# Attention scores on two halves of the matrix engine's rows, a third score buffer, and expert tiles planned around the transposes

## The chip, the cores and the metric

One core of a Trainium2 chip runs the whole kernel. The metric is the device time of one execution, in microseconds. The engines are PE (matrix multiplication; weights are loaded by PEld beside it), DVE (vector), ACT (activation functions), POOL and SP; the last two, with ACT, also issue DMAs. Matmuls write to PSUM, which has eight banks of 512 fp32 columns.

## The reference

An attention layer whose queries are pooled in pairs, followed by a layer of experts in which each row belongs to one expert, named by `domain_id`.

```python
q_pool = q.reshape(B, H, S // 2, 2, D).mean(axis=3)
scores = scale * np.matmul(q_pool, k.transpose(0, 1, 3, 2))
scores = scores - np.max(scores, axis=-1, keepdims=True)
attn = np.exp(scores)
attn = attn / (np.sum(attn, axis=-1, keepdims=True) + 1e-09)
x = np.matmul(attn, v)            # then (B, H, S/2, D) -> (B*S/2, H*D)
...
h = np.maximum(x[mask] @ w1[e], 0.0)   # for each expert e
out[mask] = h @ w2[e]
```

B = H = 8, S = 1152 keys and 576 pooled queries, D = 64; 4608 rows of 512, 8 experts with an inner width of 1024.

## The kernel before

**Attention.** Two heads make a pair; there are 32 pairs (`NPAIR`), four to a batch. The scores are computed transposed, keys on partitions, so that their exponentials are at once the stationary operand of the product with v. The 9 x 576 columns of a pair are cut into 12 steps (`SPP`) of 432 columns for both heads. `score(t)` writes a step into one of two PSUM buffers `s` (each two banks, one per head): for each head a matmul over all 128 rows, where the keys of both heads lie on the partitions (`kq`) and the queries (`qz[p % 2][r]`) are zero in the other head's 64 rows. `expo(t)` lets ACT take the exponential of both heads' 432 columns, without a maximum (reference: the rows' maximum is subtracted). `av(p, c)` multiplies one block of 128 keys with v for both heads, ten matmuls of 65 columns, the last of which holds the sum; both heads accumulate in one tile `acc` of two banks. `evac(p)` divides by the sum on DVE. `turn_k` and `turn_q` transpose k and q of the next pair on PE into the bank `tp`, from where DVE copies them.

**Experts.** When the first batches are done, their rows go to HBM (`put_x`), are gathered by expert (`get_x`, an indirect DMA on POOL, 128 rows a tile), turned and multiplied. An expert has five tiles (`NTC`, 640 slots), eight experts 40 tiles. Some tiles are computed during attention, in pieces of four matmuls of 128 columns (`up`) or one of 512 (`down`), with the bank `m`; their rows are turned by a transposing DMA (`flip_x`). The others run after it, in the tail, in `runs` of one to five tiles: `stage1` (w1 and ReLU, 32 matmuls for each stretch of columns) and `stage2` (w2, eight matmuls of 512 columns a tile), then a scatter by POOL. Runs under five tiles take their rows by `flip_x`, runs of five by `turn_tile` on PE.

**What sets the order.** The order is written out by a planner while the program is built: a loop over steps t, which issues scores, exponential, the value products that are due (`AVS`), transposes at steps 3 and 7 of a pair, and then as many expert pieces as fit: each kind of work is charged a number of nanoseconds (`C_S` 370 for a step's scores, `C_AV` 315 for ten value matmuls, `C_TK` 460, `C_TQ` 420, 216 for a piece), a step has `STEP` 769, and a piece is issued while the overrun stays under `LAG`. Each engine runs its instructions in that order. Weights of five experts (`HELD`) are loaded during attention on POOL's queue at the steps `WANT`, those of the last three in the tail. q comes by SP's queue, k and v by POOL's.

## Time and profile before

| | |
|---|---|
| median of three runs | 451.21 us (450.73 to 452.18) |
| span of the profiled execution | 456.6 us |
| attention, first to last exponential | 8.69 to 317.93 us |
| tail, from the first steady expert matmul to PE's last | 319.60 to 449.70 us |
| PE, ACT busy | 433.2, 345.8 us |
| DVE, POOL busy | 221.5, 163.3 us |
| tiles of 40 computed during attention | 6 |

The trace is one execution under the profiler. Its span, from the first to the last instruction, is the own time that it shows; it is 1.2% above the median of the runs without profiler. A row of a timeline gives the start, the time to the end of the last instruction, engine, line, operation, output and inputs and the count; in brackets the idle time before it and what ended it. PE's matmuls overlap: a row's time is longer than the distance between starts.

### The profile page before, as it was taken

The numbers are of one execution on the slowest core, as the hardware profiler recorded it, in microseconds if no ns is written. First come the engines' busy times: TensorE is split into PE (matmuls) and PEld (weight loads), VectorE is DVE, ScalarE is ACT, GpSimd is POOL, SyncE is SP. The second block draws the span as 40 slices with busy tenths as digits, with TensorE's granted clock in tenths as the row PEclk, the third lists the DMA queues.
The fourth block names the chain that finished last, engine by engine and source line by source line (L and its number), as shares of the span: only waits on it lengthen the run. The fifth ranks groups of instructions, "written<-read, shape, count | busy, mean of one in ns | idle before, by whom it ended". The sixth has DMA issues, their size and how long they took to land.

```text
span 456.6 us, 13089 instructions
## 1 busy us (share of the span) xinstructions
PE 433.2 (95%) x5568; PEld 307.1 (67%) x5568; DVE 221.5 (49%) x558; ACT 345.8 (76%) x457; POOL 163.3 (36%) x275
## 2 busy tenths in 40 slices
PE   7999999999999999999999999998979998999993
PEld 4777777777877877777777777776534545555551
DVE  4588778786554644544644554542222222333230
ACT  5999999999999999999999999998212222333221
POOL 5311241212610322644431441300646855732413
PEclk9999999999999999999999999999999999999998
DMA  8995699998999987999987799800564899941203
GB/s 204 243 249 90 109 254 228 186 243 174 184 235 234 211 147 163 231 230 235 199 170 145 158 226 210 189 13 24 140 148 134 174 244 178 236 165 71 93 8 112
DMA packets 62854, 78.61 MB, mean 172 GB/s; under 512 B 19695, under 2 KB 48880, under 8 KB 62786
## 3 DMA queue, kind: packets, MB, share of 16 engines
q0 software_dynamic: 35200, 50.31, 57.7%
q1 hardware_dynamic: 27314, 27.25, 24.6%
q8 instruction: 45, 0.74, 0.7%
q14 instruction: 23, 0.19, 0.1%
q10 hardware_dynamic: 272, 0.13, 0.1%
HBM read 95.46 MB, written 15.21 MB: 242 GB/s over the span
## 4 chain that ended last, share of the span: by engine, by line
ACT 46%; PE 31%; issue 10%; DMA 6%; POOL 4%; DVE 1%; POOLq 1%; another core or an unknown queue 1%
ACT e L599 46%; PE s L587 11%; DMA w2h<-in_moe_w_dram 6%; PE acc L610 6%; PE hp L986 5%; PE op L1019 4%; POOL out_dram L504 3%; PE acc L160 1%; PE m L768 1%; PE m L781 1%; PE tp L550 1%; PE tp L564 0%; DVE hT L993 0%; POOLq L1046 0%
## 5 line engine op out<-in xcount | busy, mean ns | idle before, releaser
L599 ACT ACTIVATE e<-s 128x864 f16<-128x864 f32 x384 | 305.9, 893 | 3.8 <-PE s L587 2.7
L587 PE MATMUL s<-qz,kq 128*128 128x432 f16 (+2 forms) x1152 | 203.1, 284 | 6.3 <-ACT e L599 4.4
L610 PEld LDWEIGHTS <-e 128*128 128x128 f16 x2880 | 120.5, 97 | 25.6 <-DVE xb L624 8.9
L610 PE MATMUL acc<-v,e 128*128 128x65 f16 x2880 | 134.3, 193 | 0.3 <-ACT e L599 0.3
L587 PEld LDWEIGHTS <-kq 128*128 128x128 f16 x1152 | 97.5, 97 | 33.0 <-issue 12.1
L504 POOL DMA_INDIRECT out_dram<-osb,gid x40 | 40.8, 1019 | 84.9 <-DVE osb L787 41.5
L111 POOL DMA_DIRECT2D vs<-in_v_dram x32 | 23.8, 743 | 114.0 <-DVE v L529 66.7
L1019 PE MATMUL op<-w2h,hT 128*128 128x512 f16 x272 | 62.1, 379 | 1.8 <-DVE hT L993 1.8
L648 POOL DMA_INDIRECT xs<-x_tok,grow x40 | 40.9, 1022 | 63.7 <-DVE xs L91 42.2
L986 PE MATMUL hp<-xt,w1h 128*128 128x384 f16 (+3 forms) x384 | 56.5, 304 | 5.6 <-issue 3.1
L986 PEld LDWEIGHTS <-w1h 128*128 128x128 f16 x416 | 36.7, 98 | 31.6 <-issue 6.0
L993 DVE TENSOR_SCALAR hT<-hp 128x384 f16<-128x384 f32 (+2 forms) x40 | 24.4, 611 | 60.1 <-PE hp L986 39.4
L571 DVE COPY qz<-tp 64x576 f16<-64x576 f16 x62 | 28.2, 456 | 51.3 <-PE tp L564 47.2
L1025 ACT COPY osb<-op 128x512 f32<-128x512 f32 x21 | 12.3, 586 | 53.1 <-PE op L1019 44.5
L991 ACT ACTIVATE hT<-hp 128x384 f16<-128x384 f32 (+2 forms) x40 | 21.2, 534 | 40.3 <-PE hp L986 35.5
L1019 PEld LDWEIGHTS <-hT 128*128 128x128 f16 x272 | 25.9, 98 | 30.6 <-DVE hT L993 2.8
L623 DVE RECIPROCAL rr<-acc 128x10 f32<-128x10 f32 x32 | 7.1, 221 | 50.6 <-PE acc L610 47.7
L520 DVE TENSOR_TENSOR qp<-q 96x768 f16<-96x768 f32 x31 | 29.3, 946 | 1.0 <-DMA q<-in_q_dram 0.9
L624 DVE TENSOR_TENSOR xb<-acc,rr 128x640 f16<-128x640 f32 x32 | 26.4, 824 | 1.1
L120 POOL DMA_DIRECT2D k<-in_k_dram x31 | 23.1, 744 | 7.0 <-DVE q L91 4.3
L1027 DVE COPY osb<-op 128x512 f32<-128x512 f32 x13 | 9.0, 692 | 32.3 <-PE op L1019 29.4
L554 DVE COPY kq<-tp 128x1024 f16<-128x1024 f16 x31 | 21.2, 683 | 3.5 <-PE tp L550 3.5
(129 smaller groups left out, 292.4 us busy)
## 6 DMA issues: line engine op xcount, KB each, us to landing
q<-in_q_dram SPq DMA_DIRECT2D x31, 576.0 KB
vs<-in_v_dram POOLq DMA_DIRECT2D x32, 288.0 KB
k<-in_k_dram POOLq DMA_DIRECT2D x31, 288.0 KB
w1h<-in_moe_w_dram POOLq DMA_DIRECT2D x16, 512.0 KB
w2h<-in_moe_w_dram POOLq DMA_DIRECT2D x16, 512.0 KB
x_tok<-xb SPq DMA_DIRECT2D x23, 96.0 KB
x_tok<-xb SPq DMA_DIRECT2D x22, 64.0 KB
x_tok<-xb SPq DMA_DIRECT2D x23, 32.0 KB
```

Source lines behind the costliest of these rows:

```text
L111: nc.gpsimd.dma_start(vs[:, :, :, :], v[b, h : h + 2].rearrange("h (p c) d -> p h c d", p=P))
L504: ins = nc.gpsimd.indirect_dma_start(out=dst[:, :], out_offset=bass.IndirectOffsetOnAxis(ap=ap, axis=0), in_=src, in_offset=None, **kw,)
L520: nc.vector.tensor_tensor(out=qp[:, :, :, :].rearrange("p j h d -> p h j d"), in0=q2[:, :, :, 0:D], in1=q2[:, :, :, D : 2 * D], op=ALU.add,)
L571: nc.vector.tensor_copy(qz[p % 2][r][lo : lo + 64, :], mt[lo : lo + 64, P : P + Sp])
L587: nc.tensor.matmul(s[:, r, o : o + n], lhsT=kq[p][:, c * P : (c + 1) * P], rhs=qz[p % 2][r][:, q0 : q0 + n], start=True, stop=True,)
L599: nc.scalar.activation(e_[:, :, o : o + W], st.pop(t)[:, :, 0:W], AF.Exp, bias=0.0, scale=0.0625)
L610: nc.tensor.matmul(acc[p][:, h, i * (D + 1) : (i + 1) * (D + 1)], lhsT=e_[:, h, o + QO[i] : o + QO[i] + P], rhs=v16[p % NV][:, c, h, 0 : D ...
L624: nc.vector.tensor_tensor(out=xb[b][:, :, 2 * hp * D : 2 * (hp + 1) * D].rearrange("p i (h d) -> p h i d", h=2), in0=a[:, :, :, 0:D], in1= ...
L648: nc.gpsimd.indirect_dma_start(out=dst, out_offset=None, in_=x_dram[0 : 1 + nb * Sp, :], in_offset=bass.IndirectOffsetOnAxis(ap=ap, axis=0),)
L986: nc.tensor.matmul(hp_[:, lo : lo + n], lhsT=w1h[:, cc, f * P : (f + 1) * P], rhs=xt[:, cc, lo : lo + n], start=cc == 0, stop=cc == ND - 1,)
L993: nc.vector.tensor_scalar(out=hT[:, f, 0:m], in0=hp_[:, 0:m], scalar1=0.0, scalar2=None, op0=ALU.max)
L1019: nc.tensor.matmul(op_[:, :], lhsT=hT[:, f, i * P : (i + 1) * P], rhs=w2h[:, f, :], start=f == 0, stop=f == NF - 1,)
```

## The change

**Scores.** `score` now issues, for each stretch of columns, one matmul on partitions 0 to 63 and one on 64 to 127 (`HALF`): each head uses its own 64 rows of the array, and the queries `qz[p % 2]` of both heads lie in one tile without zeros. Each head's result goes to its own bank. There are three `s` buffers (six banks); `acc` is one bank, used by the first head's nine blocks and then by the second's (`av(p, h, c, pool)`, `evac(p, h)`), and one bank `px` serves everything else.

**Transposes.** `turn` replaces `turn_k` and `turn_q`: 30 transposes of 64 rows, into an `s` buffer in its turn, and three DVE copies.

**Order.** Two items (two steps, or a step and a transposition) are issued as a window at the first one's step, followed by value products in groups of 15 and expert pieces. The charges are new (`C_S` 183, `C_AV` 147 for five, `C_T` 440, `C_P` 217, and `C_MODE` 190 for a window), with exceptions for the windows around the transposes (`SPAN`).

**Experts.** Five experts (`FILL`) instead of three have tiles filled in; rows are turned on PE in attention (`turn_x`) and in the tail. Six experts' weights are held, the sixth in space that q's load buffers leave (`wlast`); the last two are loaded two pieces a run. q of the pairs from the fifth on is loaded by POOL's queue, one pair earlier.

**Checks.** The reciprocals of all sums are kept; `check_sums` counts on the chip those out of a range, and if any is, a general path (`again`) recomputes all with the rows' maxima. It lies behind a branch at the program's end, where there was one for experts with over 640 rows.

```diff
-    NFX = 14
+    NFX = 10
...
-    ering = att.enter_context(tc.tile_pool(name="ering", bufs=3))
+    ering = att.enter_context(tc.tile_pool(name="ering", bufs=4))
...
-    spsum = att.enter_context(tc.tile_pool(name="spsum", bufs=2, space=bass.MemoryType.PSUM))
+    spsum = att.enter_context(tc.tile_pool(name="spsum", bufs=3, space=bass.MemoryType.PSUM))
     apsum = att.enter_context(tc.tile_pool(name="apsum", bufs=1, space=bass.MemoryType.PSUM))
-    tpsum = att.enter_context(tc.tile_pool(name="tpsum", bufs=1, space=bass.MemoryType.PSUM))
-    mpsum = att.enter_context(tc.tile_pool(name="mpsum", bufs=1, space=bass.MemoryType.PSUM))
+    xps = att.enter_context(tc.tile_pool(name="xps", bufs=1, space=bass.MemoryType.PSUM))
...
-            nc.sync.dma_start(
+            (nc.sync if p < 4 else nc.gpsimd).dma_start(
...
+    def turn(p):
+        kp, qp = kpt[p], qpt[p]
+        new_kq(p)
+        mt = spsum.tile([P, 2, 512], FP32, name="s")[:, :, :].bitcast(F16)
+        for c in range(NC + NJ):
+            src = kp[:, c, :, :] if c < NC else qp[:, c - NC, :, :]
+            for r, (lo, hi) in enumerate(HALF):
+                nc.tensor.transpose(
+                    mt[:, r, c * 64 : c * 64 + 64],
+                    in_=src[lo:hi, :, :].rearrange("p h d -> p (h d)"),
+                    identity=ident16[lo:hi, lo:hi],
+                )
...
-            for r in range(2):
+            for r, (lo, hi) in enumerate(HALF):
                 nc.tensor.matmul(
-                    s[:, r, o : o + n], lhsT=kq[p][:, c * P : (c + 1) * P],
-                    rhs=qz[p % 2][r][:, q0 : q0 + n], start=True, stop=True,
+                    s[:, r, o : o + n], lhsT=kq[p][lo:hi, c * P : (c + 1) * P],
+                    rhs=qz[p % 2][lo:hi, q0 : q0 + n], start=True, stop=True,
                 )
...
+    WSTEP = [[20 + 44 * e + 11 * j for j in range(4)] for e in range(4)]
+    WSTEP.append([236 + 13 * j for j in range(4)])
+    WSTEP.append([(NPAIR - 3) * SPP + 10 + 3 * j for j in range(4)])
...
+    AVS = [
+        {at: [(g // 3, c, ACC) for c in range(3 * (g % 3), 3 * (g % 3) + 3)] for g, at in enumerate(ats)}
+        for ats in ((9, 11, 13, 15, 17, 19), (9, 11, 13, 15, 16, 19))
+    ]
+    AVS_END = {
+        8: [(0, c, ACC) for c in range(4)],
+        10: [(0, c, ACC) for c in range(4, 6)],
+        12: [(0, c, ACC) for c in range(6, NC)],
+        13: [(1, c, ACC) for c in range(NC)],
+    }
+    STEP, C_MODE, C_S, C_T, C_AV, C_X, C_P, LAG = 771, 190, 183, 440, 147, 220, 217, 250
+    SPAN = ({2: 1270, 4: 1700, 5: 880}, {3: 1200, 5: 1500, 6: 1150})
+    FILL, HELD = 5, len(WSTEP)
...
+        def able(self, t):
+            b = self.blocks[0] if self.blocks else None
+            return b and (b[3] or b[4].get("t", NST) < t < NST - 14 and t >= WSTEP[b[4]["xs"][0]][3] + 14)
...
-    for e, i in [(e, i) for i in range(NA) for e in range(HELD - 2)]:
+    early = [(0, 0), (1, 0), (2, 0), (3, 0), (0, 1), (1, 1), (2, 1), (3, 1), (4, 0), (4, 1)]
+    for e, i in early + [(e, 2) for e in range(FILL)]:
         add_tile(e, i)
...
+        if s_ == (10 if p == 0 else 7 if p == 1 else 4) and p + 1 < NPAIR:
+            items.append(-(p + 1))
+    windows = {}
+    for i in range(0, len(items), 2):
+        w = items[i : i + 2]
+        windows[w[0] if w[0] >= 0 else w[1]] = w
...
+        for it in windows.get(t, ()):
+            if it < 0:
+                turn(-it)
+                work_ns += C_T
+            else:
+                score(it)
+                expo(it)
+                work_ns += C_S
+                span += STEP
+        if span:
+            work_ns += C_MODE
+            span = SPAN[p % 2].get(s_, span) if p > 1 else span
...
+            room = (180 if p > 1 and s_ in SPAN[p % 2] else LAG) + span - debt - work_ns
...
-                if j1 - j0 < NTC:
-                    flip_x(dst, en, j)
-                else:
-                    btw.append(lambda dst=dst, j=j: turn_tile(dst, xs[en, j], j))
+                btw.append(lambda dst=dst, en=en, j=j: turn_tile(dst, xs[en, j], j))
...
+        h = stage1(wts[e][0], xt[k_], n * P, {**at, 2: part, 7: part})
...
+        if k_ == 3:
+            check_sums()
+        if i1 == NTC and e in (0, 3) and rest:
```

PE, in the middle of attention (pair 17 and about). Before, one expert matmul (`m<-w2h`), then a step's scores and the first transpose:

```order
L610 LDWEIGHTS e
L610 MATMUL acc<-v_1_104,e 128x65
L781 LDWEIGHTS h_4043
L781 MATMUL m<-w2h,h_4043 128x512
L587 LDWEIGHTS kq
L587 MATMUL s<-qz_0_99,kq 128x432
L587 LDWEIGHTS kq
L587 MATMUL s<-qz_1_100,kq 128x432
L550 LDWEIGHTS kp
L550 MATMUL tp<-ident_106,kp 128x128
```

After, at a like place, a window of two steps (the last of one pair, the first of the next), with the buffers' numbers kept:

```order
L814 LDWEIGHTS h0_4866
L814 MATMUL px_5108<-w2h_1377,h0_4866 128x512
L594 LDWEIGHTS kq_4723
L594 MATMUL s_5118<-qz_0_96,kq_4723 128x432
L594 LDWEIGHTS kq_4723
L594 MATMUL s_5118<-qz_0_96,kq_4723 128x432
L594 LDWEIGHTS kq_4975
L594 MATMUL s_5122<-qz_1_97,kq_4975 128x432
L594 LDWEIGHTS kq_4975
L594 MATMUL s_5122<-qz_1_97,kq_4975 128x432
L615 LDWEIGHTS e_4973
L615 MATMUL acc_5092<-v16_0_100,e_4973 128x65
```

Two steps' scores stand together, both halves of a step read the same q tile, and value products and expert matmuls lie between windows.

DVE, at the transposes of a pair. Before, the evacuation of both heads (`rr`, `xb`), then the copies of k (`kq`) and of the zero-padded q (`qz`):

```order
L623 RECIPROCAL rr<-acc 128x10
L624 TENSOR_TENSOR xb<-acc,rr 128x2x5x64
L91 MEMSET xs 1x1
L554 COPY kq<-tp 128x1024
L571 COPY qz_0_101<-tp 64x576
L571 COPY qz_1_102<-tp 64x576
L572 COPY kq<-tp 128x128
```

After, for one head (its sums' reciprocals are kept in `cum`), then the copies from a score buffer:

```order
L628 RECIPROCAL cum<-acc 128x5
L630 TENSOR_TENSOR xb<-acc,cum 128x5x64
L570 COPY kq<-s 128x2x9x64
L575 COPY qz_97<-s 128x6x64
L575 COPY qz_97<-s 128x6x32
```

The evacuation is half as wide and comes twice a pair, and the three copies free a score buffer.

ACT, from the last exponential into the tail; `hT<-hp` is ReLU, its columns the run's rows, `osb<-op` a finished tile, `xt<-hp` turned rows. Before:

```order
L599 ACTIVATE e<-s 128x2x432 x384
L991 ACTIVATE hT<-hp 128x384 x4
L1025 COPY osb_7117<-op 128x512
L1025 COPY osb_7147<-op 128x512
L991 ACTIVATE hT<-hp 128x384 x4
```

After:

```order
L606 ACTIVATE e<-s 128x2x432 x384
L1048 ACTIVATE hT<-hp 128x384 x4
L1082 COPY osb_8037<-op 128x512
L1082 COPY osb_8067<-op 128x512
L1048 ACTIVATE hT<-hp 128x128 x4
L1082 COPY osb_8150<-op 128x512
L1048 ACTIVATE hT<-hp 128x128 x4
L1067 COPY xt<-hp 128x4x128
L1082 COPY osb_8239<-op 128x512
L1048 ACTIVATE hT<-hp 128x256 x4
```

Before, five runs of three tiles, two of two and three of five follow; after, one of three, two of one, six of two and two of five.

## Rows read from the trace of the kernel before

**Rows 1.** The page's first line.

```profile
span 456.6 us, 13089 instructions
```

**Rows 2.** Three windows: stretch, length, busy time (count) by engine, clock, DMA.

```profile
19.08:113.37 94.29, 92.14 (x1458) 71.97 (x1455) 73.82 (x224) 94.29 (x121) 21.53 (x32) 1.00 0.98 195
113.37:317.90 204.53, 201.68 (x3203) 158.07 (x3199) 100.84 (x218) 201.91 (x253) 66.47 (x101) 1.00 0.90 179
319.60:449.70 130.10, 122.45 (x744) 65.98 (x744) 36.51 (x80) 35.59 (x67) 65.60 (x118) 1.00 0.63 146
```

**Rows 3.** Timeline: start, time, engine, line, operation; POOL and ACT at a stall.

```profile
289.09 1.02 POOL L648 DMA_INDIRECT xs<-x_tok,grow  x1 [0.27 <-issue]
...
290.56 1.67 ACT L599 ACTIVATE e<-s 128x864 f16<-128x864 f32 x2 [0.66 <-PE s L587]
```

**Rows 4.** Groups by shape, 100 to 200 us: count, busy us, mean ns, idle before.

```profile
L587 PE MATMUL s<-qz,kq 128*128 128x432 f16 x126 | 33.1, 344 | 0.8 <-ACT e L599 0.4
```

**Rows 5.** Timeline of PE around 153 us.

```profile
152.30 0.47 PE L610 MATMUL acc<-v,e 128*128 128x65 f16 x10
...
152.61 0.38 PE L768 MATMUL m<-xt,w1h 128*128 128x128 f16 x4
...
152.83 0.53 PE L587 MATMUL s<-qz,kq 128*128 128x288 f16 x4
...
153.50 0.53 PE L587 MATMUL s<-qz,kq 128*128 128x432 f16 x2
...
153.87 0.61 PE L550 MATMUL tp<-ident,kp 128*128 128x128 f16 x8
...
154.34 0.53 PE L587 MATMUL s<-qz,kq 128*128 128x432 f16 x2
```

**Rows 6.** Timeline of PE in the tail, one row for each width.

```profile
343.25 5.36 PE L986 MATMUL hp<-xt,w1h 128*128 128x384 f16 x32
...
376.55 1.69 PE L986 MATMUL hp<-xt,w1h 128*128 128x256 f16 x14
...
403.89 0.39 PE L1004 MATMUL hp<-ident,xs 128*128 128x128 f16 x4
...
440.78 8.80 PE L1019 MATMUL op<-w2h,hT 128*128 128x512 f16 x40
```

**Rows 7.** Groups by shape, 318 to 457 us: the closing matmuls.

```profile
L1019 PE MATMUL op<-w2h,hT 128*128 128x512 f16 x272 | 62.1, 379 | 1.8 <-DVE hT L993 1.8
```

**Rows 8.** Timeline of PE in the tail's second run.

```profile
333.90 0.81 PE L986 MATMUL hp<-xt,w1h 128*128 128x384 f16 x4 [1.78 <-issue]
335.29 0.81 PE L986 MATMUL hp<-xt,w1h 128*128 128x384 f16 x4 [0.58 <-issue]
336.77 1.46 PE L986 MATMUL hp<-xt,w1h 128*128 128x384 f16 x8 [0.68 <-DVE xs L91]
```

**Rows 9.** Timeline at the end of attention.

```profile
316.25 1.68 ACT L599 ACTIVATE e<-s 128x864 f16<-128x864 f32 x2
...
317.99 0.45 PE L610 MATMUL acc<-v,e 128*128 128x65 f16 x9 [0.34 <-ACT e L599]
...
318.27 0.81 PE L986 MATMUL hp<-xf,w1h 128*128 128x384 f16 x4
...
318.73 0.82 DVE L624 TENSOR_TENSOR xb<-acc,rr 128x640 f16<-128x640 f32 x1
...
319.61 0.66 PE L986 MATMUL hp<-xf,w1h 128*128 128x384 f16 x3 [0.52 <-DVE xb L624]
```

**Rows 10.** Groups, 100 to 317 us (DVE's copies); whole span (POOL's loads of k).

```profile
L571 DVE COPY qz<-tp 64x576 f16<-64x576 f16 x44 | 20.0, 456 | 44.2 <-PE tp L564 42.8 <-PE m L454 0.8
...
L554 DVE COPY kq<-tp 128x1024 f16<-128x1024 f16 x21 | 14.4, 684 | 0.0
L572 DVE COPY kq<-tp 128x128 f16<-128x128 f16 x22 | 4.9, 225 | 0.6
...
L120 POOL DMA_DIRECT2D k<-in_k_dram x31 | 23.1, 744 | 7.0 <-DVE q L91 4.3
```

More of the change, by code (lines that the diff above doesn't have):

```diff
@@ L935 @@
             room = ROOM[s_]
-            while rq and room > 0 and rq[0][0] <= room:
-                cost, fn = rq.pop(0)
+            while rq and room > 0 and rq[0][0] <= room and not (len(mmq) > 1 and rq[0][2:]):
+                cost, fn = rq.pop(0)[:2]
                 room -= cost
```

487 lines of the change are left out of this document (311 added, 176 removed).

## The prediction

> **What bounds the kernel now.** I read the page first, then the busy time by stretch, then the matrix engine's order of time inside one stretch of each kind. The span is 456.6 us [rows 1]. The windows cut it in three [rows 2]: attention before any expert work is filled in (19.08 to 113.37 us), attention with filling (to 317.90), and the expert stage alone, the tail (319.60 to 449.70). In the first, ACT is busy all the time: 120 exponentials start in 94.29 us (the 121st that is counted reaches in), one per 0.786 us, and PE, also nearly full by its busy share, hides under it. In the second, 252 (counted in the same way) take 204.53 us, 0.812 each. What ends ACT's waits there is PE: [rows 3] shows a wait of 0.66 us for scores while a gather ran on POOL. So there both engines bound. In the tail PE alone bounds; 130.1 us for 34 tiles (272 closing matmuls at eight a tile [rows 7]).
>
> Durations of matmuls overlap, so costs are taken from distances between starts. One step's scores, two of 432 columns, hold PE 0.37 us (153.50 to 153.87); ten value matmuls 0.31 (152.30 to 152.61); four expert matmuls of 128 columns 0.22; eight transposes 0.47 [rows 5]. In the tail [rows 6] a start-to-start is 0.216 us at 512 columns (8.80 less the last one's 0.38, by 39), 0.162 at 384, 0.109 at 256 (1.69 less 0.273, by 13) and 0.056 at 128.
>
> **The change, part by part.**
>
> *Fewer tiles in the tail.* The order shows 13 tiles filled into attention (52 transposes of gathered rows, four a tile) where six were, so the tail has 216 closing matmuls, 27 tiles. PE's work in the tail before: five runs of three tiles, 5 x 32 x 0.162 = 25.9; two of two, 2 x 32 x 0.109 = 7.0; three of five, 3 x 32 x (0.216 + 0.056) = 26.1; 272 x 0.216 = 58.8; 60 transposes x 0.056 = 3.4; in all 121.1 us. After: one run of three, 5.2; two of one, 64 x 0.056 = 3.6; six of two, 20.9; two of five, 17.4; 216 x 0.216 = 46.7; 96 transposes, 5.4; in all 99.1. **Term 1: -22.0 us**, all on the path, since PE bounds there.
>
> *Waits in the tail.* 130.1 less 121.1 leaves 9.0 us in which PE waits. Of these 1.78 + 0.58 + 0.68 = 3.0 us stand in the second run [rows 8], whose input came by transposing DMAs, which the tail no longer issues. **Term 2: -3.0.** The bounds: 0, if the smaller runs wait as much at their borders, and -4.8, which is the whole tail shrunk in proportion (7 x 130.1 / 34 = 26.8 for both terms). Weights of the last two experts are issued two pieces a run instead of four at once; POOL is busy 65.60 of 130.1 us, and the next expert needs them three runs later, so I cost that at nothing.
>
> *End of attention.* Before, the last exponential ends at 317.93; nine value matmuls follow, four expert matmuls start at 318.27, and PE stands until 319.61 for the evacuation [rows 9]. After, five value matmuls of the first head, its evacuation (about 0.7 us: half of 0.82 plus the reciprocal and two handovers) and then 45 value matmuls of the second head, 45 x 0.031 = 1.4, follow that exponential, since one accumulator bank serves both heads in turn. The first expert matmul needs no bank of theirs any more. Start about 2.5 us after the exponential; before, counting the four early matmuls at their 0.65, effectively 1.0. **Term 3: +1.5.**
>
> *The pace of attention.* Twelve steps and one set of transposes make a pair of heads; ACT's floor for it is 12 x 0.786 = 9.43 us. PE's work for it before: 12 x 0.37 + 90 x 0.031 + 15 transposes x 0.059 = 8.1, and the six tiles add about 1.0: nearly full, hence 0.812. After: no row shows two matmuls on separate halves of the array's rows. Both bounds come from the rows: a score step holds PE 0.184 us if the halves run wholly side by side and 0.37 if in line. I take 0.184, because the two halves share neither rows of the array, nor operands' partitions, nor a PSUM bank, and because the planner's charges for the old steps (370, 315) are what [rows 5] shows, which makes its 183 a believable estimate. Passing from half-height matmuls to full ones and back, which the planner charges with 190 ns a window (`C_MODE`), has no row either; the nearest is that a 432-column matmul is modelled at 344 ns [rows 4] while its successor starts 184 later, so some 160 ns of filling and emptying: 0 to 0.32 us for a window, in and out, of which I take 0.19, about the middle. Thirty half transposes cost 0.44 (planner) to 0.94 (30 x 0.031); I take 0.44. With 6.5 windows a pair: 2.2 + 2.8 + 0.44 + 1.24 = 6.7 us, and 13 tiles at 32 x 0.056 + 8 x 0.216 + 0.22 = 3.73 over some 22 pairs add 2.2: 8.9 of 9.43, about 0.5 us spare a pair, 11 us in all. The third score buffer lets ACT run on through a late PE for one more step, more than the 0.66 us of [rows 3]. So ACT could return to 0.786 throughout: 252 x 0.026 = -6.5 us. I keep a part back, since filling is still planned up to the brim of a window. **Term 4: -4.0**, bounds -6.5 and, by the rival on switching below, +8.
>
> The Trainium skill bears on the first of these costs. "TensorE: Matmul & The Clock Gate" (Part 3, Measured speedup vs the span model) reports 3.07 times for four row tiles of the array, which falls short of four. In that proportion two halves would gain 1.54 times; an estimate from it puts a step at 0.24 us, 0.055 x 264 = 14.5 us more in the filled pairs against 11 spare, so Term 4 at +3.5 and the whole at 431 us. No row of this trace shows it.
>
> *Work hidden at no cost.* DVE's copies after the transposes were 0.684 + 2 x 0.456 + 0.225 = 1.8 us a pair; by the rate of [rows 10] the three new ones are about 1.3, and the buffer that they free is next written two windows later, over 2 us of cover; if DVE came later than that, PE would stand with everything behind it. The evacuation is split in two, 0.4 us more in a pair for a DVE busy 100.84 of 204.53 us. Loads of q move from SP's queue to POOL's: 28 x 0.744 = 21 us of issue time [rows 10], in front of gathers, scatters and weights; POOL is busy 66.47 of 204.53, q now comes a pair earlier, and each expert piece waits at least 14 steps after its weights. The sixth expert's weights are issued 17 to 26 steps before the end; 17 x 0.786 = 13 us cover. The check of the sums is five short DVE operations and one matmul, and the general path is an untaken branch where another stood.
>
> **Sum:** -22.0 - 3.0 + 1.5 - 4.0 = -27.5, so a span of 429.1. The median of the runs, 451.21, is 0.988 of this execution's span; the same ratio gives **424.0 us**.
>
> **Rivals.**
>
> *Switching costs more.* If every window pays 0.32 us, 0.13 x 6.5 x 22 = 18.6 us more are wanted of PE, 11 are spare, 8 lengthen attention and Term 4's gain goes: 456.6 - 23.5 + 8 = 441, or 436 us. For it: every window has both kinds of matmuls, one after the other. Against: filling that began before the next set of scores would overlap part of it. The Trainium skill speaks for it: "TensorEngine Tiling (Array Packing)" (Key Properties) says that a change of tiling mode drains TensorE. The trace has no such change in it.
>
> *The halves run in line.* This is the slower side. A step costs 0.37: 12 x 0.186 x 22 = 49 us more, 11 spare, so attention grows by 38 and does not gain 4: 424 + 42 = 466 us. It decides from 27.5 + 11 - 4 = 34.5 us over 264 steps, 0.13 a step: at about 0.315 us a step and above, the kernel is slower than before. It is also the way in which the change would not do what it says. Against it: the operands are on disjoint partitions and the results in separate banks.
>
> *The gain is larger.* ACT at 0.786 throughout, the tail shrunk in proportion, and the wait for the first head's evacuation covered (+0.8): -26.8 + 0.8 - 6.5 = -32.5, 419 us. For it: nothing in the tail but PE's work and its waits.
>
> **How the numbers follow.** Forecast with its own spread, 413 to 432: 0.71 (the larger gain is within it). Switching, 432 to 443: 0.13. Between that and the old time, 443 to 450: 0.05, when both unknown costs lie above the middle. In line, or near it, over 452: 0.06. No change: 0.02. Below 413: 0.03. A range of 412 to 442 leaves out about two in ten. What a measurement can tell from no change is about 0.3%, 1.4 us. Faster 0.92, same 0.02, slower 0.06.
>
> **What would show it.** Right: score matmuls of the two halves start within a few tens of ns of each other and a pair of them holds PE under 0.2 us; exponentials one per 0.79 us from 113 us on; expert matmuls of the tail starting about 2.5 us after the last exponential; a tail of about 105 us for 27 tiles. Wrong: 0.37 us for the pair of halves; PE idle of over 0.2 us at each border between scores and value matmuls; ACT waiting for scores in most windows; PE in the tail waiting for weights or gathered rows. A changed pace in the first 113 us would say that the transposes in the score buffers, not the filling, hold ACT up.

## The result, and the profile after

The changed kernel takes 438.98 us (436.93 to 440.12, four runs), the kernel before 451.69 beside it (450.73 to 452.63): a ratio of 0.971 (0.967 to 0.975), 12.7 us less. The forecast was 424.0. Faster was right; the gain is under half of the 27 us foretold.

One thing has to be known for all that follows. Runs of one comparison share a chip, and as far as six comparisons show, chips are of two kinds for this program. In this comparison and in one later (chip 9) the kernel before takes 452 us; in four others (chips 10, 4, 15, and 10 again) its medians are 458 to 461. I call them chips A and B; only chip 10 was seen twice, so whether it is the chip that divides them, or something else that lasted through a comparison, is not shown. The trace of before that the prediction used, 456.6 us long [rows 1], is of kind B by its time and its late signals (below), as is each of the three that I took later (455.4 to 459.4). The trace of the changed kernel below is of kind A. On B the changed kernel has a ratio of only 0.993 (0.990 to 0.996).

The page's first line, to be set beside [rows 1]; this execution took 440.12 us:

```profile
span 438.1 us, 14671 instructions
```

Three windows of the changed kernel, as [rows 2], cut at the first exponential of pair 2, of pair 10, and the end of attention (stretch, length, busy time and count by engine, clock, DMA):

```profile
31.45:107.34 75.89, 64.30 (x1300) 42.06 (x1297) 58.30 (x197) 75.62 (x96) 23.84 (x35) 1.00 0.99 194
107.34:324.13 216.79, 209.15 (x3979) 139.51 (x3975) 117.09 (x286) 211.24 (x265) 92.76 (x142) 1.00 0.92 188
327.76:430.01 102.25, 101.00 (x733) 62.16 (x730) 36.45 (x95) 32.57 (x69) 53.36 (x97) 1.00 0.50 124
```

The tail is 102.25 us for 27 tiles, with PE busy in 101.00 of them, 3 us less than the 105 of the forecast. Attention went the other way. Pair 2 begins at 31.45 us, against 28.51 in before's trace, and the 264 exponentials of pairs 10 to 31 take 216.79 us, against 213.97. Attention ends 6.2 us later than before's, where it was to end 4 us earlier.

The halves do what they were meant to do. PE's timeline around 119 us, to be read beside [rows 5]:

```profile
118.05 0.81 PE L814 MATMUL px<-w2h,h 128*128 128x512 f16 x3
118.79 0.54 PE L594 MATMUL s<-qz,kq 64*128 64x432 f16 x4
119.26 0.63 PE L615 MATMUL acc<-v,e 128*128 128x65 f16 x15
```

From 118.79 to 119.26 two steps' scores, four matmuls, and the way back to full height take 0.47 us. At 0.184 a step that leaves 0.10 for the change of mode on the way back. The way in stands before them: the three matmuls of 512 columns need 0.65 us by [rows 6], and the scores start 0.74 us after the first of them, 0.09 later. The change of mode is 0.19 us a window in all, the value that Term 4 had taken.

ACT now waits in the wake of the transposes. An even pair, unfilled (PE, DVE and ACT):

```profile
90.91 0.36 PE L594 MATMUL s<-qz,kq 64*128 64x432 f16 x2
...
91.10 0.42 PE L565 MATMUL s<-ident,kp 64*128 64x64 f16 x18
...
91.63 0.63 PE L615 MATMUL acc<-v,e 128*128 128x65 f16 x15
...
92.19 0.55 PE L594 MATMUL s<-qz,kq 64*128 64x144 f16 x8
92.59 0.89 ACT L606 ACTIVATE e<-s 128x864 f16<-128x864 f32 x1 [0.27 <-PE s L594]
```

Between the scores at 90.91 and the next at 92.19 stand the 30 half transposes and 15 value matmuls, which the table gives to step 16 of the odd pair before (step 4 of this one). From distances between exponentials, less 0.770 us each, even pairs lose 0.28 us at step 4 unfilled and 0.32 filled; filled odd pairs lose 0.12 at step 4, 0.28 at step 5 and 0.30 at step 7, unfilled odd ones 0.11 at step 7. In sum: 4.6 us in pairs 0 and 1, 2.0 in 2 to 9, 12.5 in 10 to 30. Before: 1.3, 1.5 and 10.3.

A filled odd pair:

```profile
198.26 0.35 PE L594 MATMUL s<-qz,kq 64*128 64x144 f16 x4
198.46 0.76 DVE L570 COPY kq<-s 128x1152 f16<-128x1152 f16 x1 [1.72 <-PE s L565]
...
199.14 0.51 DVE L575 COPY qz<-s 128x384 f16<-128x384 f16 x2
...
199.64 0.54 PE L594 MATMUL s<-qz,kq 64*128 64x288 f16 x6
200.04 2.63 ACT L606 ACTIVATE e<-s 128x864 f16<-128x864 f32 x3 [0.33 <-PE s L594]
```

The transposes write a score buffer from 197.81, and it is free when the copies end at 199.65, 1.84 us or 2.4 exponentials later. The third buffer is lent out just then. The loan alone makes no stall: it is as long, 1.84 us, in the unfilled odd pairs.

Pair 1's stall (DVE and PE), the longest of all, 2.66 us between two exponentials:

```profile
24.30 1.99 DVE L212 CAST dal<-dom 32x8 f32<-32x8 int32 x9
...
24.86 0.36 PE L565 MATMUL s<-ident,qp 64*128 64x64 f16 x12
...
26.30 0.76 DVE L570 COPY kq<-s 128x1152 f16<-128x1152 f16 x1
26.97 0.51 DVE L575 COPY qz<-s 128x384 f16<-128x384 f16 x2
...
27.62 0.49 DVE L630 TENSOR_TENSOR xb<-acc,rr 128x320 f16<-128x320 f32 x1
...
28.17 0.93 PE L615 MATMUL acc<-v,e 128*128 128x65 f16 x15 [1.64 <-DVE xb L630]
```

Nine casts of the routing run on DVE until 26.29 while the transposes have been done since 25.22; the evacuation comes after the copies, and PE stands for it, with all that ACT needs behind it.

The end of attention, as [rows 9]:

```profile
324.18 0.30 PE L615 MATMUL acc<-v,e 128*128 128x65 f16 x4 [0.49 <-ACT e L606]
324.52 0.19 DVE L628 RECIPROCAL cum<-acc 128x5 f32<-128x5 f32 x1 [3.42 <-PE acc L615]
324.75 0.49 DVE L630 TENSOR_TENSOR xb<-acc,cum 128x320 f16<-128x320 f32 x1
325.29 2.65 PE L615 MATMUL acc<-v,e 128*128 128x65 f16 x45 [0.81 <-DVE xb L630]
327.76 2.07 PE L1043 MATMUL hp<-xf,w1h 128*128 128x384 f16 x9
```

The first matmul of the tail starts 3.6 us after the last exponential, not 2.5. The 45 value matmuls take 2.47 us to the next start, 55 ns each instead of the 31 of [rows 5], because the granted clock has fallen. Windows of the changed kernel (columns as above, the clock third from the end):

```profile
12.00:16.00 4.00, 2.73 (x40) 1.66 (x39) 0.97 (x4) 4.00 (x6) 0.00 (x0) 0.83 1.10 232
16.00:22.00 6.00, 4.96 (x76) 3.02 (x70) 3.16 (x10) 4.92 (x7) 4.43 (x6) 0.54 1.16 237
...
26.00:32.00 6.00, 4.26 (x60) 2.65 (x58) 5.23 (x17) 4.01 (x6) 1.03 (x2) 0.72 1.16 238
...
324.00:328.00 4.00, 3.00 (x50) 2.78 (x51) 0.70 (x3) 0.13 (x1) 0.00 (x0) 0.66 0.02 4
```

Both levels stand in these stretches, 1.2 GHz for most of 16 to 22 us. In before's trace the clock was 1.00 at the start:

```profile
12.00:16.00 4.00, 3.52 (x62) 2.75 (x58) 1.56 (x4) 3.83 (x6) 0.00 (x0) 1.00 1.14 254
```

At the end of attention the clock of the changed kernel is 0.66 after waits of 0.49 and 0.81 us. The Trainium skill has a mechanism of this kind ("TensorE: Matmul & The Clock Gate", HAM oscillation): a wait for data after a short burst of matmuls throttles the clock, and the next burst starts slow. For waits as short as these the runs do not bear it out: in the runs nofill and full (below) the same two waits stand there, and the 45 value matmuls run at full clock. So why the clock falls here stays open. In nofill's timeline:

```profile
316.22 1.53 PE L615 MATMUL acc<-v,e 128*128 128x65 f16 x45 [0.81 <-DVE xb L630]
```

### The profile page after: what moved, and what is told of

It reads as the page before. It is cut to its first block, busy times and chain, and to the rows that moved or that the text cites. A ratio compares the mean times of both kernels' runs of the same rounds, so it can differ in the third digit from the quotient of the medians.

```text
span 438.1 us, 14671 instructions
## 1 busy us (share of the span) xinstructions
PE 400.2 (91%) x6346; PEld 260.7 (60%) x6346; DVE 230.6 (53%) x644; ACT 342.9 (78%) x460; POOL 184.1 (42%) x304
## 5 line engine op out<-in xcount | busy, mean ns | idle before, releaser
L594 PE MATMUL s<-qz,kq 64*128 64x432 f16 (+2 forms) x1152 | 122.7, 290 | 18.0 <-ACT e L606 13.4
L615 PEld LDWEIGHTS <-e 128*128 128x128 f16 x2880 | 102.5, 99 | 43.4 <-issue 18.5
L594 PEld LDWEIGHTS <-kq 64*128 64x128 f16 x1152 | 45.8, 94 | 61.6 <-issue 42.0
L655 POOL DMA_INDIRECT xs<-x_tok,grow x40 | 40.5, 1012 | 91.6 <-DVE xs L93 34.7
L1043 PEld LDWEIGHTS <-w1h 128*128 128x128 f16 x416 | 35.9, 98 | 16.1 <-issue 2.6
L1043 PE MATMUL hp<-xt,w1h 128*128 128x256 f16 (+2 forms) x384 | 44.1, 273 | 0.4 <-ACT hT L1048 0.4
L1050 DVE TENSOR_SCALAR hT<-hp 128x256 f16<-128x256 f32 (+3 forms) x44 | 21.3, 485 | 40.9 <-PE hp L1043 24.7
L1048 ACT ACTIVATE hT<-hp 128x256 f16<-128x256 f32 (+3 forms) x44 | 18.8, 432 | 28.5 <-PE hp L1043 23.1
L570 DVE COPY kq<-s 128x1152 f16<-128x1152 f16 x31 | 23.5, 758 | 28.8 <-PE s L565 27.9
L801 PE MATMUL px<-xt,w1h 128*128 128x128 f16 x416 | 32.9, 220 | 0.0
L814 PE MATMUL px<-w2h,h 128*128 128x512 f16 x104 | 30.4, 382 | 0.0
L801 PEld LDWEIGHTS <-w1h 128*128 128x128 f16 x416 | 23.9, 98 | 5.9 <-issue 5.9
L806 DVE TENSOR_SCALAR h<-px 128x512 f16<-128x512 f32 x26 | 17.9, 688 | 17.0 <-PE px L801 17.0
```

Source lines behind the costliest of these rows:

```text
L570: nc.vector.tensor_copy(kq[p][:, :].rearrange("p (c r k) -> p r c k", c=NC, r=2), mt[:, :, 0 : NC * 64].rearrange("p r (c k) -> p r c k", ...
L594: nc.tensor.matmul(s[:, r, o : o + n], lhsT=kq[p][lo:hi, c * P : (c + 1) * P], rhs=qz[p % 2][lo:hi, q0 : q0 + n], start=True, stop=True,)
L615: nc.tensor.matmul(acc[p, h][:, i * (D + 1) : (i + 1) * (D + 1)], lhsT=et[p, c // 3][:, h, o : o + P], rhs=v16[p % NV][:, c, h, 0 : D + 1] ...
L655: nc.gpsimd.indirect_dma_start(out=dst, out_offset=None, in_=x_dram[0 : 1 + nb * Sp, :], in_offset=bass.IndirectOffsetOnAxis(ap=ap, axis=0),)
L801: nc.tensor.matmul(m[:, f % 4, :], lhsT=wts[e][0][:, cc, f * P : (f + 1) * P], rhs=h0["xt"][:, cc, :], start=cc == 0, stop=cc == ND - 1,)
L814: nc.tensor.matmul(h0["o"][:, :], lhsT=h0["h"][:, f, :], rhs=wts[e][1][:, f, :], start=f == 0, stop=f == NF - 1,)
```

## The experiments

Each edit is on the changed kernel unless it says otherwise. "Excess" is the sum of the distances between starts of exponentials, less 0.770 each; "lost in the tail" is the sum of the distances between starts of matmuls from the last exponential on, less what [rows 6] and [rows 5] give for their widths.

### Chip 10 (B): three single edits

> The kernel before, unchanged, to have a second trace of it. Theory A (the first profile of before, span 456.6 us, was a usual execution): span near 456 again, tail of about 131.6 us from the last exponential to PE's last matmul. Theory B (that execution was longer than usual, as the medians say: 451.7 us, and after's profiles read 2 us below its times): span near 450, and the tail or attention about 6 us shorter; the sum of the prediction then started from a base with about 6 us of waits too many.

458.69 us, span 456.6, attention ending at 316.5, 12.2 us lost in the tail. So the trace behind the prediction was no oddity, but of a program that takes 459 us there, not 451.

```diff
-        10: [(0, c, ACC) for c in range(4, 6)],
-        12: [(0, c, ACC) for c in range(6, NC)],
-        13: [(1, c, ACC) for c in range(NC)],
+        10: [(0, c, ACC) for c in range(4, 6)] + [(1, c, (xps, "px")) for c in range(6)],
+        12: [(h_, c, (ACC, (xps, "px"))[h_]) for c in range(6, NC) for h_ in range(2)],
```

> The changed kernel, with the last pair's second head accumulated in the bank px beside the first head's acc, so that only ten value matmuls follow the last exponential instead of five, an evacuation and 45. Theory A (the transition at the end of attention costs what the trace shows: 3.6 us from the last exponential to the first tail matmul, then twelve matmuls at the half clock): first tail matmul about 1.0 us after the last exponential, granted clock stays at 1.0, kernel 2.5 to 4 us faster than the changed one (439.0), about 435.5. Theory B (the tail is held by something else, gathers or weights): PE waits later by as much, no gain.

455.0 us, 0.991 of before. The end of attention in this kernel's timeline:

```profile
330.80 0.30 PE L615 MATMUL acc<-v,e 128*128 128x65 f16 x4 [0.24 <-ACT e L606]
330.94 0.31 PE L615 MATMUL px<-v,e 128*128 128x65 f16 x5
...
331.39 1.79 PE L1042 MATMUL hp<-xf,w1h 128*128 128x384 f16 x10
```

The last exponential ends at 330.75, the tail starts 0.64 us later: 3.0 us of the transition are saved. From the last exponential to the last matmul 115.5 us pass, against 118.3 in av17's trace from the same chip.

```diff
-        for ats in ((9, 11, 13, 15, 17, 19), (9, 11, 13, 15, 16, 19))
+        for ats in ((9, 11, 13, 15, 17, 19), (9, 11, 13, 15, 17, 19))
```

> The changed kernel with one entry of the table of value products moved: the group that odd pairs had at step 16 (step 4 of the next pair, directly behind the transposes) goes to step 17, behind the next window's scores. Theory A (ACT starves at step 4 of even pairs because PE has 15 value matmuls between the transposes and the next scores, no buffer is missing): the mean excess of the interval after step 4 in even pairs falls from 0.32 us to under 0.1, 15 pairs x 0.25 = 3 to 4 us less attention, unless it reappears at step 5 or 6. Theory B (the transposes hold one of three score buffers, so ACT starves whatever PE's order): the excess stays within 0.1 us of 0.32.

455.98 us, 0.992. In the timeline the scores now come straight after the transposes, and the values behind them:

```profile
90.75 0.34 PE L565 MATMUL s<-ident,qp 64*128 64x64 f16 x12
...
90.98 0.36 PE L594 MATMUL s<-qz,kq 64*128 64x144 f16 x4
...
92.06 0.62 PE L615 MATMUL acc<-v,e 128*128 128x65 f16 x15
```

In unfilled even pairs the 0.28 us at step 4 fall to 0.00 (0.06 come back at step 6, 0.11 at step 1); in filled ones 0.23 stay. So the order of PE's work makes that stall, as far as no expert piece is there. Little is won by it: the excess of pairs 10 to 30 is 17.9 us, where the changed kernel's two traces from chips B have 18.7 and 19.5.

```diff
+        if t < 22 and span:
+            dummies(5)
+        if t in (21, NST):
+            dummies(6)
```

> The changed kernel with idle matmuls of zeros into a free bank, in the windows of the first two pairs and while PE waits at the end of attention; nothing else moves. Theory A (PE does less since the halves run side by side, the granted clock falls to 0.57 in 14 to 22 us and 0.54 in 325 to 328, and this is what the first two pairs and the end lose): granted clock 1.0 in these stretches, pair 2 begins near 29 to 30 us instead of 31.45, the 45 value matmuls at the end take 1.4 instead of 2.4 us; 2 to 4 us faster than 439.0. Theory B (the first pairs wait for loads and for DVE, the clock is only a symptom): pair 2 still begins at about 31 us, and only about 1.5 us at the end are won.

(`dummies(n)` multiplies spare data, 288 columns, into the spare bank; seven more stand after the first head's last evacuation.) 457.86 us, 0.995. The clock stays at full level at the start, and pair 2 begins at 30.80, no earlier than in the two others (30.53, 30.71). Either five such matmuls a window take as much of PE as the clock gives back, or DVE's order sets the start; this run does not tell. At the end of attention the clock stays at full level too: the 45 value matmuls take 1.39 us, and the tail starts 2.56 us after the last exponential, not 3.63.

By their times none of the three is told from the changed kernel, whose ratio is 0.993 (0.990 to 0.996) on such chips; what they show stands in their traces.

### Chip 4 (B): the changed kernel, full height, DVE's order, four edits

> The changed kernel itself, so that the single edits can be set against it on one chip. If its gain doesn't hang on the chip: a ratio near 0.971 to the kernel before, last exponential 6 us later than before's, PE losing about 4.5 us in the tail. If the 16 us that its variants lost in the tail belong to the chip: a ratio near 0.995 and 15 to 17 us lost there.

457.83 us, 0.993; 16.8 us lost in the tail, attention ending at 329.7. So both numbers, which the variants had too, do not come from their edits.

```diff
-  lhsT=kq[p][lo:hi, c * P : (c + 1) * P], rhs=qz[p % 2][lo:hi, q0 : q0 + n],
+  lhsT=kq[p][:, c * P : (c + 1) * P], rhs=qz[p % 2][:, q0 : q0 + n],
```

> Only the score matmuls are changed: both of a step are read from all 128 rows (so that every score is the sum over both heads; this is the part of the computation that differs), and they stand in line at 0.37 us a step; the planner and the order stay. If halves side by side give back 0.186 us a step and the change of mode costs nothing: 12 x 0.186 = 2.2 us a pair more work, 0.5 us of it spare, over the 21 filled pairs about +36 us on the changed kernel, a ratio to it near 1.08. If each window also paid 0.19 us for the change of mode, 1.2 us a pair come back: +10 us, 1.02. If the halves gain nothing: no difference.

466.8 us, 1.012 of before and 9.0 us over the changed kernel: near the second number, and for its reason. PE's timeline of this kernel:

```profile
117.57 0.81 PE L814 MATMUL px<-w2h,h 128*128 128x512 f16 x3
118.22 0.89 PE L594 MATMUL s<-qz,kq 128*128 128x432 f16 x4
118.95 0.62 PE L615 MATMUL acc<-v,e 128*128 128x65 f16 x15
```

The scores of two steps take 0.73 us instead of 0.47, and start 0.65 us after the first of the three matmuls ahead of them instead of 0.74. So the halves save 0.26 us a window and pay 0.09 of it for the way in: 0.17 net, some 1.1 us of PE's time a pair. Excess in pairs 10 to 30 rises from 18.7 to 28.7, 0.48 us a pair: the rest, 0.6, was spare, near the 0.5 that the prediction reckoned. And full height keeps the clock at the start at 1.00 (12 to 32 us) and the excess of pairs 0 and 1 at 2.4 instead of 3.5.

```diff
-        if t >= 12:
+        if t >= 24:
             room = ROOM[s_]
```

> The routing pieces on DVE begin one pair later (step 24 instead of 12). If DVE, busy with them while the transposes wait to be copied, makes the stall in pair 1: the interval of 2.66 us between two exponentials there falls to 1.2 to 1.6 us and attention ends 1 to 2 us earlier. If the matrix engine or the loads make it: the interval stays, and the time within 0.5 us of the changed kernel.

456.32 us, 1.5 less than the changed kernel. The interval in pair 1 falls from 2.64 to 1.12 us; the copy starts as soon as the transposes are done:

```profile
25.29 0.35 PE L565 MATMUL s<-ident,qp 64*128 64x64 f16 x12
...
25.68 0.76 DVE L570 COPY kq<-s 128x1152 f16<-128x1152 f16 x1 [2.68 <-PE s L565]
```

So DVE's order made that stall. Attention ends only 0.3 us earlier in the trace (329.4): in this execution the clock was at 0.50 from 16 to 22 us, and intervals of 1.47, 1.41, 0.99 and 1.41 stand there.

Four edits in one: the ones of end_px, av17 and rt24, and `check_sums` cut in two, its matmul put one run later.

> Four edits on the changed kernel: an even pair's value matmuls moved from step 16 to 17, the last pair's second head accumulated in the spare bank, routing pieces a pair later, and the matmul of the sums' control one run later. If each takes away the stall it is aimed at: about 2 + 3 + 1 + 1.5 = 7.5 us less than the changed kernel, a ratio to before of 0.955. If the stalls only move to the next late engine: within 2 us of the changed kernel.

450.08 us, 0.976 of before (0.971 to 0.982), 7.75 less than the changed kernel. Attention ends 2.9 us earlier, and from there to the last matmul 113.1 us pass instead of 118.1. Of these 5.0 the transition has 2.9; I put the rest down to the sums' control, which no run has alone.

### Chip 9 (A): what the chip adds, and three tables

```diff
-            scatter(out, osb[:, :], ids(i), "oscat", N - 1)
+            nc.sync.dma_start(dump[d_ * P : (d_ + 1) * P, :], osb[:, :])
...
-        gather(x_[:, :], grow[:, e * NTC + i : e * NTC + i + 1], nb[0])
+        nc.sync.dma_start(x_[:, :], x_dram[lo : lo + P, :])        # tail only
```

> In the tail alone the indirect gathers and scatters are replaced by plain transfers of whole blocks on SP's queue, as many bytes (so the tail's rows are not those of their expert, and the result of the tail goes to a scratch area; this is the part of the computation that is changed). In the changed kernel's trace of 457.8 us the matrix engine lost 16.8 us in the tail, and 15 of its 16 late signals there (0.26 to 3.6 us after the matmul's end) have an indirect DMA on POOL running or just over. If these hold the signals up: under 6 us lost in the tail and about 11 us less time, a ratio near 0.970 where before takes 459 us. If dense short matmuls or the matrix engine itself make the delay: 16 us lost as before, 0.99. Where before takes 452 us, no delays are to be taken away, and both give 0.97.

436.97 us, 0.963 (0.958 to 0.969), with 4.1 us lost in the tail. This was a chip A, and settles nothing; the same kernel ran again on a B (below).

> The four edits of the last run and four matmuls of 288 columns on spare data in each window of pair 0, so that the granted clock doesn't fall at the start. If the half clock at 12 to 22 us is what is left of the late start: pair 2 begins at 28.5 us instead of 29.5, about 1 us less, a ratio of 0.974 where before takes 461. If the loads or DVE set the start: pair 2 at 29.5 or later, 0.976 or above.

The four edits of combo1 and one more: `if 2 <= t < 14 and span: dummies(4)`. 433.19 us, 0.956 (0.950 to 0.961). Pair 2 begins at 28.88, the clock is 1.00 from 8 to 32 us; in combo1, without the spare matmuls, pair 2 began at 29.48, and at 28.77 with them on a chip B (combo2_b), so the clock was worth about 0.6 us there. In this trace attention ends at 320.98 and 2.7 us are lost in the tail; the page's first line:

```profile
span 431.4 us, 14730 instructions
```

```diff
-    SPAN = ({2: 1270, 4: 1700, 5: 880}, {3: 1200, 5: 1500, 6: 1150})
+    SPAN = ({4: 1540}, {})
```

> The same, and the planner's table of window lengths is cut to one entry (turn window of even pairs 1540), so that the same 13 tiles are filled in, but no window of an odd pair is given more than its own length plus 0.25 us. If overfilled windows of odd pairs make ACT's stalls there (12 us over ten pairs): 5 to 8 us less in pairs 10 to 30 and in the time. If it is the amount of work in a pair whatever its place: within 1 us of the version with the old table.

436.10 us, 2.9 more than combo2. Excess in pairs 10 to 30 is 16.0 against 11.9; odd pairs keep 9.2 against 8.0. So my theory of overfilled windows falls: the old table is the better one.

```diff
-        alone = [e for e in range(FILL) if done.get(e, 0) == NA - 1][-2:]
+        alone = [e for e in range(FILL) if done.get(e, 0) == NA - 1][:0]
```

> The same as the second, and the two runs of one tile at the head of the tail are joined to those of two tiles of the same experts, so that nine runs are left of eleven and the matrix engine's work stays within 0.2 us. If the delays of 6 to 7 us belong to the short runs: 4 to 7 us less where before takes 459 us. If they only move to the next run, or the next run waits for gathered rows: within 2 us, or up to 4 us more.

436.91 us, 3.7 more than combo2. The timeline shows why the short runs are there:

```profile
332.64 0.40 PE L1069 MATMUL hp<-ident,xs 128*128 128x128 f16 x4 [3.51 <-DMA xs<-x_tok,grow]
```

Without them the second run's rows are wanted 3.5 us before they are there.

### Chip 15 (B): the cause on chips B, and the price of filling

> The kernel before once more, for its trace beside the others of this call. Its two traces so far (456.6 us) have 17 and 20 matmuls of which the signal comes over 0.25 us late and 10.5 and 12.2 us of lost matrix-engine time in the tail. If chips differ in this and the chip is one on which it takes 452 us: no late signals, 3 to 5 us lost, a span near 450. On one where it takes 459 us: as in the two traces.

461.4 us, span 459.4, 21 late signals (signals of PE that come 0.25 us or more after their matmul's recorded end), 13.2 us lost in the tail.

> The changed kernel once more. Where before takes 452 us: a ratio of 0.971, no late signals, 4.5 us lost in the tail. Where it takes 459 us: 0.993, some 40 late signals and 16 us lost.

455.46 us, 0.993 (0.990 to 0.996), 41 late signals, 15.8 us lost.

> Plain block transfers in place of the tail's indirect gathers and scatters, as in the run called plain (the tail's rows are not those of their expert; its result goes to a scratch area). Where before takes 459 us: if POOL's indirect DMAs hold the matrix engine's signals up, under 6 us are lost in the tail and the time is about 11 us under the changed kernel's; if not, 16 us and within 2 us of it. Where before takes 452 us: within 3 us of the changed kernel (it was 0.9634 to 0.9711), which settles nothing.

444.14 us, 0.967 (0.963 to 0.971): 11.3 less than the changed kernel beside it, 11 foretold. The tail of the changed kernel on this chip, and of this variant:

```profile
334.70:448.25 113.55, 104.11 (x733) 62.84 (x730) 36.41 (x95) 32.80 (x69) 53.52 (x97) 0.97 0.46 111
```

```profile
333.39:436.28 102.89, 101.71 (x733) 62.44 (x730) 36.32 (x95) 32.57 (x69) 8.55 (x13) 0.99 0.51 132
```

113.55 us become 102.89, near what a chip A takes with the indirect DMAs in place (102.25). That it is the indirect kind, and not POOL's DMAs at large, no run separates: POOL is busy for 53.52 us in the one tail and 8.55 in the other. Part of the loss is the clock's. After the late signals it stands at half in the changed kernel's tail, and at 1.00 in the variant's over the same stretch:

```profile
352.40:359.10 6.70, 3.75 (x15) 1.83 (x15) 0.93 (x4) 0.55 (x2) 2.41 (x6) 0.50 0.25 72
```

What such a delay looks like, in the changed kernel's timeline on this chip:

```profile
348.80 0.38 PE L1043 MATMUL hp<-xt,w1h 128*128 128x128 f16 x4 [1.00 <-issue]
349.05 1.01 POOL L515 DMA_INDIRECT out_dram<-osb,gid  x1 [0.27 <-issue]
349.89 0.28 ACT L1048 ACTIVATE hT<-hp 128x128 f16<-128x128 f32 x1 [2.53 <-PE hp L1043]
...
350.22 0.38 PE L1043 MATMUL hp<-xt,w1h 128*128 128x128 f16 x4 [1.04 <-ACT hT L1048]
350.36 0.98 POOL L515 DMA_INDIRECT out_dram<-osb,gid  x1 [0.24 <-ACT hT L1048]
351.32 0.29 DVE L1050 TENSOR_SCALAR hT<-hp 128x128 f16<-128x128 f32 x1 [2.57 <-PE hp L1043]
```

Four matmuls that the records end at 349.18 are followed by PE's signal at 349.87, those of 350.60 at 351.30, 0.19 and 0.04 us before POOL's indirect DMA ends by its record (350.06, 351.34). ACT and DVE sit idle for it, and PE, out of buffers, for them. In the variant 20 such matmuls run in one row:

```profile
346.99 1.37 PE L1047 MATMUL hp<-xt,w1h 128*128 128x128 f16 x20 [0.18 <-ACT hT L1052]
```

I set each of PE's signals in a trace against the recorded end of the matmul before it, up to the kernel's last matmul, and call it late from 0.25 us on. On chips A (five traces) there is none; on B there are 30 to 46 in the nine other traces of the changed kernel and its variants, but only 8 in nofill (below). In this variant 24 are left, all in attention, where its indirect DMAs remain. Of the 39 in the changed kernel's trace from chip 4, 29 have an indirect DMA on POOL in progress between matmul and signal. By chance it would be 9, as 23% of all signals have one in progress just behind the matmul, or about 14 if stretches as long as the late ones are set behind other signals.

> No expert tile is filled into attention: all 40 are left to the tail. If filling makes ACT's stalls in pairs 10 to 30 (12 us over the floor of 0.770 us an exponential): they fall to what the unfilled pairs 2 to 9 have, 0.25 us a pair, 5 us in all, and attention ends near 317 us. If the transposes alone make them, filled or not: 10 us or more stay and it ends at 322 or later. The tail grows by 13 tiles x 3.65 = 47 us, about 480 us in all where before takes 452.

488.69 us. Excess in pairs 10 to 30 is 4.6, attention ends at 315.06. The windows of pairs 10 to 31 and of the tail:

```profile
106.18:315.06 208.88, 171.83 (x3407) 110.71 (x3403) 87.50 (x223) 208.33 (x265) 60.47 (x90) 1.00 0.85 165
317.82:477.92 160.10, 150.97 (x981) 81.23 (x981) 48.54 (x113) 44.36 (x74) 80.76 (x149) 0.98 0.42 111
```

Filling makes the odd pairs' stalls (1.2 us left in ten of them); the even pairs' 3.4 stand at step 4, where av17 shows the order of PE's work. Attention is 216.79 on A and 223.72 on B with filling, so against the 208.88 here 13 tiles cost 8 and 15 us there, 0.6 and 1.1 a tile, and they save 46.6 in the tail (160.10 less 113.55), 3.6 a tile. Filling pays on either. The 8 late signals are few for a tail with 13 more tiles of indirect DMAs on a chip B; three of them stand in one stretch, 6.5 to 6.7 us after a matmul's end at 332.3. So the number of these DMAs alone does not set how many signals come late.

### Chip 10 again (B)

> The kernel before once more, for a trace of a chip on which it takes 452 us, if this is one: then no late signals, 3 to 6 us of matrix-engine time lost in the tail instead of 10 to 13, a span near 450 and attention ending at 315 to 317. If late signals are not what divides the chips: as many as before (17 to 24), and the difference of 8 us elsewhere.

457.49 us, span 455.4, 10.2 us lost: again a B. So there is no trace of before from a chip A, and where its 7 us between the kinds stand is not shown.

> The version with the four edits and the matmuls on spare data in pair 0, once more beside before. It had a ratio of 0.956 where before takes 452 us, and should have it again there. Where before takes 459 us, the changed kernel lost 12 us of its gain to late signals, which none of the five edits touches: about 0.974, near that of the four edits alone (0.976).

449.59 us, 0.980 (0.975 to 0.985), with 41 late signals; the 0.976 of the four edits alone lies within that. Faster than both kernels on either kind of chip, by more on A.

## Why the prediction missed

Against the span of before's trace, which the sum stood on:

The transition counts from 1.0 us after before's last exponential, as in the forecast.

| part | forecast | in the trace of after (A) | in after_b's (B) |
|---|---|---|---|
| Terms 1 and 2, the tail | -25.0 | -28.4 | -17.1 |
| Term 3, end of attention | +1.5 | +2.6 | +2.6 |
| Term 4, attention | -4.0 | +6.2 | +13.2 |
| after the last matmul | 0 | +1.1 | +1.0 |
| span | -27.5 | -18.5 | -0.3 |

Before's trace is from a chip B. So the third column sets a chip A against a B, and that its tail comes out better than forecast owes something to the chip; the last column sets B against B.

Nine of the fifteen us of error stand in the third column; the other six are the scaling of the span to the median by 0.988 (429.1 to 424.0, where after's median lies 0.9 above its span). The 1.1 us after the last matmul I did not pursue.

**Term 1 was right.** 99.1 us of PE's work were forecast for 27 tiles; the tail took 102.25 on a chip A, 2.9 of it waits.

**Term 2 had the wrong cause.** I put the waits of [rows 8] down to the transposing DMAs. In the second trace of before the like wait (2.7 us at 330) begins with signals of PE that come 2.7 us late, and another 2.9 us stand at 398. In the first trace, which has 14 late signals, none is recorded in that stretch; but DVE takes up a matmul's result there 2.5 us after its recorded end (333.29 after 330.81), so I count these waits among them. In the changed kernel, whose tail has no transposing DMA, they are gone on a chip A and stand on a B: 16 to 17 us lost there, against 10 to 13 before. This is also most of the answer to why 12.7 us on one chip are 3 on another: the changed kernel takes 16 to 19 us more on a B, 11 of them in the tail, where plain_b takes them away, and 7 in attention, where some 25 of its 40 late signals stand and no run takes them away. The changed kernel's shorter runs leave less cover for a late signal, an explanation that I only argue.

**The base was in part counted twice.** I read the difference between the execution of the trace and the medians as a slower pace of everything, and took 1.2% off. It was another kind of chip, with waits at single places, and those of [rows 8], which Term 2 had already taken away, are among them. How the rest of the 7 us is spread no trace of before from a chip A shows. An execution 7 us over the medians should have been asked where these 7 us stand.

**Term 3 was too small by 1.1** because the 45 value matmuls ran at 55 ns, not 31, at the fallen clock; in warm, with the clock at full level, they took 1.39 us, the 1.4 of the forecast. I had priced them from a busy stretch.

**Term 4 had the wrong sign**, and it is the step that failed: attention was to be 4.0 us shorter and became 6.2 longer. It has three parts. The start, +2.9: nothing in my working looked at pairs 0 and 1. There the clock fell, where PE with half-height scores was less busy (2.73 of the 4 us from 12 to 16, against 3.52 in before's trace), and at full height or with spare matmuls it did not; and DVE came late to the transposes, which I had named as the condition ("if DVE came later than that, PE would stand with everything behind it") and not looked up. rt24 and combo2 take both away: pair 2 at 28.88. The unfilled pairs, +0.4: no change, as forecast. The filled pairs, +2.8 instead of -4: most of their stalls, 8.2 of 12.5 us, stand in odd pairs, and without filling those lose 1.2; the even pairs' stand at step 4, behind the value matmuls. PE's work itself was priced about right, 0.19 us for a window's change of mode and some 0.6 spare in a pair. What failed is that it was priced by the mean of a pair, while ACT waits near the transposes, where value matmuls and expert pieces stand before the next scores; the table of windows fills to the brim, which the prediction saw. That the spare half microsecond lies in other windows is argued, and combo2_a3, which fills odd pairs' windows less, did not mend it. The sentence "The third score buffer lets ACT run on through a late PE for one more step" overlooked that the transposes now live in that pool, so that at each turn the third buffer is gone for 1.84 us. That this adds to the stalls of the filled pairs is argued too, since the loan is as long in pairs that lose little.

**The rivals.** Switching was priced at 0.32 us a window for the costlier case, and Term 4 took 0.19; 0.09 on the way in and 0.10 on the way back are what the rows leave, so this rival fell. That the time lies in its band, 432 to 443, is chance. The Trainium skill ("TensorEngine Tiling (Array Packing)", Key Properties) says that a change of mode drains TensorE; the trace agrees, with 0.1 us at either border. The estimate of 0.24 us a step did not come out: two steps hold PE 0.47, and 0.37 without the way back. Nor did the halves run in line. The full-height run comes near that slower side, 466.8 us and slower than before, but it is not that rival itself: it also saves the change of mode, which halves in line would still pay. For the rival I counted +42; for the run the expectation had +10, and +9.0 came. By the same token the halves themselves are worth 9 us on a chip B in this order of work, and not more.

## What to carry to other kernels

When a resource becomes cheaper, look for the places where it was waited for, not at its mean: 1.1 us of PE's time a pair became 0.5 us, because the rest was spare and ACT waits mostly near the transposes, where the order of the work decides. A mode that has to be entered and left costs at both borders; read the row before the scores as well as the one behind. And before a trace is scaled to a median, ask at which places it is longer; two traces of the same program from two chips tell that at once.

## What the runs showed of the hardware

- PE's signals can come 0.3 to 3.6 us (6.7 once, in nofill) after the recorded end of a matmul, most often while POOL works on an indirect DMA, on some chips (10, 4, 15) and not on those of kind A; POOL's DMAs themselves are as long on both (1012 and 1018 ns for a gather). With the half clock that follows them (0.50 from 352.4 to 359.1 us in after_b) such delays cost 11 us in a tail of 103. What divides the chips stays open, and so does the way by which POOL holds the signal up.
- Two 64-row matmuls of 432 columns on separate halves run side by side nearly without loss: two steps and the way back to full height take 0.47 us, and the way in 0.09, against 0.73 in line at full height.
- The granted clock fell to half for a while between 11 and 24 us in all ten traces with half-height scores and no spare matmuls at the start (0.54 from 16 to 22 us in after's). In none of the others did it fall there: one at full height, five with four or five matmuls on spare data a window, four of the kernel before.
